# Three units in the first group of each exponential phase, in a kernel that runs window attention beside a feed-forward product

## The chip, the cores and the metric

One core of a Trainium2 chip runs the kernel. The time is the device time of one execution in microseconds, and lower is better. Three runs of the kernel before lie between 299.94 and 300.24 us, with a median of 300.06 us. The core has TensorE (PE in the profile, with its weight load PEld), VectorE (DVE), ScalarE (ACT), GpSimd (POOL) and SyncE (SP); the last two mainly issue transfers here.

## The reference

Attention over 8 batches of 8 heads, 576 positions and 64 numbers a head: each position sees itself and the 127 before it, with a bias that grows with distance by a slope of the head. The result, 4608 rows of 512, goes through `h = x @ w_in` (2048 wide), `g = h * cos(h)` and `g @ w_out`.

```python
scores = scale * np.matmul(q, k.transpose(0, 1, 3, 2))
mask = (rel >= 0) & (rel < window)                # window = 128
scores = np.where(mask, scores + bias[None], -1000000000.0)
...
attn = attn / (np.sum(attn, axis=-1, keepdims=True) + 1e-09)
x = np.matmul(attn, v) ...                        # 4608 x 512
h = x @ w_in
g = h * np.cos(h)
return (g @ w_out).astype(np.float32)
```

## The kernel before

The program is written as a list of operations, each with what it reads and writes. The operations of one engine run in an order that a table gives: `Plan.follow(TABLE)` unpacks a string into steps of 16 bits, one for each operation, and builds the order from them. For an operation that either ACT or DVE can do, the high bit says which. Semaphore waits come from what an operation reads and writes, so nothing runs ahead of its data, and an operation that waits holds up what is behind it on its engine.

The attention is cut into units. A unit (b, pair, G) is a batch, a pair of heads and one half (G = 0 or 1) of the first 512 positions; a unit (b, 't') is the last 64 positions of a batch for all heads. There are 72. Nine are done at the start. The rest is spread over six phases, which have 8, 10, 10, 12, 14 and 9 units; in each phase ACT loads the table of the exponential once, does the phase's units, and goes back to the cosine. Between and beside them run the feed-forward products of a block of 512 rows a phase.

A group of units goes through these steps:

- `scores` (L539, and L529 for a 't' unit): PE writes q·k of a unit into two banks of PSUM. One run holds the scores of all units of the group.
- `exps` (L598, L590): ACT takes the exponential of a unit into `p` or `ptail`.
- `mask` (L623, L611): DVE multiplies by `emask`, which holds bias and window (made by ACT at L460 from `dif`, which POOL makes).
- `pv` (L653, L656; L640, L642): PE multiplies by v into one bank of PSUM a unit.
- `norm` (L694, L696; L681, L684): DVE divides by the sums and writes `xnats`; in phase 5 `norm_two` (L710, L712) divides two units' sums at once.
- x is then transposed, either on PE (L742, into the bank that held the unit's sums, and copied out by ACT L752 or DVE L753 into `xT`) or by a DMA on SP.

The eight banks of PSUM are dealt out by name: 4 to 7 are `SB` (scores, and the first product of the feed-forward part), 2 and 3 are `UB` (sums with v, and the transposes of x), 0 and 1 are `OB` (second product). With two units in a group the scores take all four of `SB`.

The first product is L782 (L975 for the first block), its cosine is L787 on ACT and its product h·cos(h), `gT`, is L791 on DVE. The second product is L1161 (first block) and L1067; L1067 works on 256 columns and on sums `wsum` and `gsum` besides. Its results are copied from PSUM by ACT (L1052) or DVE (L1053) into `ob` and stored by SP. At the start, q and k of batch 0 are loaded, transposed on PE (L483) and copied into `qt` and `kt` by ACT (L500) and DVE (L501). From batch 2 on they are loaded by POOL and transposed by DMAs on SP (L396, L399). v is loaded at L375, `w_in` at L407, `w_out` at L413.

Of the kernel before, what the change touches and what calls it, by code (L numbers as in the profile page):

```python
# [37 lines left out]
    '!JB(zEKr!Mj%{>;HUNYjab!Z7$qCql;L3G!CjefR+FFk(bw73vr<2ntCbb8MB)_5dQYyf6J%<J=0tY;ul(MgN&rc'
    'O0s&EiG$uIcm#Y~Vab;v#yqnaVrE7GY>V-A}Btqa`;P_Nv&jvF#{*7WM`>VMkre&#)Wy?uO_aV#gax-'
    'm{4=v5trFP6j>R?Tw2c0rY#J*M(j<PaOY>o)>#w^hUa2)xJ2kX>J~-'  # L40
    '#3SczLYEI#)13`0UMgZCvSU&r@KXVhQx8AYHOt^~S#t385v1pL)39f1&X4(!RY_VSn%~;N7Le~0Vt5k)3C!7qncH'
    'Sb_KKyP6<WQBL=(H{om`}^2hwehkBNkN1f6-'
    '=6Jf`#n1*9F&|{#~8ip5b`?XFO3>mnmKg4fqM&X#D2BXTu`vb#MxEL-'
    '2=FZh<=U!>)?uhVjo~ev?pC0h90j^d!W2#$W>Vg}3Lez;yMB~`dF58D5!*GHZ4bkokcrZJo8XMBIs3+J`c0!*&!='
    'cNak2M(+9t6%k<c;_TI5&xT-;_~SjMe)zLQ?kr-'
    '9G)}so_oZgT~!nS)>B%(>F{i(nL<%Kma6dPT_kIY8xqVGm@6sSZY)QY;}3kyZHF!JjrNbPWohF6A1kpQae^Jz>4Y'
    'nMq|4ag_#Z%abX$X0Qx{bdg5-'
    'w!C^Sy0wzSSv6YO*7!5g5KOZPW>L)jeqDWi^PVfHiNt_&bV&I7<#pb?el1f*R3lvbBscPqQM6(|M=#E!7MQtWiEo'
    '^$q8jetWg{{laSk`ID;w6<lHL!It@CI3ZRWxET-dy=6bdfZi^BN)-'
    'kx6rkxYh^Af7Y$CX%W0qP@nf!;+_cuy#JAV$$(>L5)aS8M@n1a32RRL3Yb{W0a`!VJ8|o4{JEnxs(L});p(&v8a9'  # L50
    'u_yO{KZHL$YuW?tu(Sy-'
    '!vCGTmAdZpg4wXLtycpkG<<E5@OtDZg=!_1h1+Njmjw*z0aL)7QnhFOPv(elHPlI>oe%EXgvk}suL+RHI+l!oPEe'
    'ttc)y)KY7q-'
    'GO9HpEp~!82*s>_!_J5TR{@5f%EL7h^Wh(4l4fbO%j~jd783&`#My06C4>3;+Is6L%3tT|^hYe#$tr1&iB&6{dwW'
    'wmj!;Baz_4=p8Jja_9ps>tY{=<;GUvOwSAXGq+K`;>!KNrH|ImXY(ASTzHFN^apdvpSj*r6^VK)$8H@P=`NPcPO&'
    'XkYSBhFw`irt0gqb!LQPqlVQC7VwU?z)4yP6n<)+6xUk=rH29r)HJ=#nkkufV0J5o_@v9wsQWd0@&P$WT0e*0vOC'
    'WIl=#9la*x}LDtWaQG=0xl2(#f%Kz3QWi+K|tR$xwKh#_K~ywPUk>V_~X988-'
    'dL$7M*|kTUzrMQ~>ttJm@GYT>9QFLiQ#JGHIu^Q5UX9joXGsV+1N~s5tf4rg&Z0t843@yK)VUZ;eO{vvf>bj#_<{'
    'E{YJE13lG{)N}UY3D6Y>lsCkRX4ja{$9_e$IQETy;j`zD56VwIGwJ{vRRhIkkY72;<?OL;WxyDsbjLJ`d?#gik4L'
    '%OwvOj>3X-Yk5pe`ia}jeHouYwjx-lYe?zUO*6w~{=z!E<7?VOdoJcyIBk3;YN22T&Udsl*?z2EoT*eN`VQ(2lOw'  # L60
    '$ie!%Cd#CND}y^H-5G~apWoVM#%(x$>q1=4UeA7@v$>FHVpXpRNz-`z1w9-2S&rNI|0<^yIkuIxJ1&2qr-'
    'yn-P&*BAkwbEg<YgZWM`B<Ux7!?;yxT0hEB9Poq9_H<xB+6$<+&1*V*jXQ=!i##UhbBC-HxJ9b4f>O5FQM$GVlYY'
    '0;EzOMeT$+Oi@ir?~G>em;QF`Fb7Uw0-'
    ')DSUv5QX5E;wvHsQX@ok50m+CO*%wR0XM0gH$JNq(o?|pd}rcrfU%@Ny^NS$EwY}9WNlRrb}CwAb0!CyUIkX8zeE'
    't`lBMNi5`Z9289jS-byN0#8`Z0-K46!6u51NJvfI*I<pVOKD}#Bep<(EjKAJ>#OvyA?}aT-'
    'Eb<QtZWG>gAiq@nZu|-Z>5YIIxXgTPJ-Qv8(%8OF{x~utj?J<T~4~q=Mu!G!`B%o{U^X7EYfMjy|cFw5l`KlR}P!'
    'Ka8_mW<8uzKs|eA|5Ic*_e7cdlcU3q+K^v!GU5I4-4igxj^A<ASLge=;<iQSZL!w7=WR?W#-'
    'vXhCLeN@7x(>g+{qRDABl6lLS<Fw>!h`LQKaFe(HMu)ipAva=P&;AW;|7_8}?>Xa&1&CWqRI3oTyJm0VHkMj~b-'
    'KU~R;VLVn(IO$x|2XD-#Cwa~YvoxGM@0FUnOnlZXB(9|3jhMQu{ARUV7(DVnyPJ@o)_f&pP-'
    '0v1&I@q5tK0fHEZqW2B6vpePz;Nsr3p!)OwvLraMQ%IB0%b!Fk8kvD!^ICX(d5SU`>)JBl;A)3x!^A~*gA1H!Njk'  # L70
    '9bb31AJ#9jLnSFn5nJP8V+>6WI*{{9$K=-'
    'Ii4(}ekB>9rlTbz8;dAV@$vsGY#Mm*p3)v9cI)0mEeyn;9Sk1Ej+_{IEB=6m(OWM%qp|L4FkV=POcUwRSz4?%tjO'
    '!EE7%nJVFo1y$1xLEKDW3+%V*`a_(LEi!<eA{Ja22J?)4@RI|7PRIIN8a6UkTIrQNx^0MmIX}Gdse33v8*ibI3(}'
    'Q6!`hQq7VFL0TWDyL%1z)LEb|Fqa2QJsRyz<9M$)jGC(Gyq6mu#GUiIyWiMn}lrw_vC^2CnX65Kq(JOA5auqsW#('
    'az6gPr;3Fs3vS*iFTO!lleCE-fW~K`s@;f-'
    'DuL7*vWwMFvwo)YDYK%Ys!&lL=}a$qa_Dqe_$j$%4|P%7Sk&C^p7|E-05OoaEoQU{w(_HKhuIl)N)0L6E?If-ndQ'
    'f>bOkomPRMj6=zXYB;2Fs8S$=8>KAS9bxj%$jo92RQykW$_h$ynL-'
    ';1n|B~0C{NjJ5M;#~HD{_qDyS92ASr8Q=(}$hf?wlN8Dh7U35CEE3Rb4eZHcVrLB=YO&ys+EVM&F9-'
    '>_E|awkyN8>TE$>Y^ZLfm%hXRv?#4)t*Y5EYzr4%5w1xWK3uw7gWYn<tfyI;9|8HRZ>;#t145fwkp%W<gb}oO8Vt'
    ';%~TDI391Zd3iT@kVuEmcuME+!AOkCeh?Xh408{MGRAGcvK=>2_;SOCz;Xi5FXBMh@##BcNK~)Hu608vNLvl*BDH'  # L80
# [15 lines left out]
class Plan:  # L96
# [63 lines left out]
    def follow(self, text):  # L160


        raw = zlib.decompress(base64.b85decode(text))
        n, at, self.order = len(raw) // 2, 0, []
        assert n == len(self.all)
        for lo, hi in zip(raw[:n], raw[n:]):
            at = (at + lo + 256 * hi) % 65536
            o = self.all[at % 32768]
            if isinstance(o.fn, dict):
                e = "dve" if at >= 32768 else "act"  # L170
                o.fn, o.eng = o.fn[e], (e,)
            self.order.append(o)
# [80 lines left out]
def bass_alibi_sliding__then__act_gcu_kernel(  # L253
# [8 lines left out]
    with ExitStack() as ctx:  # L262
# [12 lines left out]
        JN, PRE2, SEEDN, XD, LORD = (5,), (), {}, {4: 6}, 0  # L275
        SDPRI, NH, LWPRI, G1, S4IN, SPLIT = 1, 2, 2, 1, True, True
# [3 lines left out]
        SB, UB, OB = [4, 5, 6, 7], [2, 3], [0, 1]  # L280

# [236 lines left out]
        def scores(us, slot):  # L518

            def f(e):  # L520
                ins = None
                for n, (b, pr, G) in enumerate(us, slot):
                    banks = SB[2 * n:2 * n + 2]
# [21 lines left out]
            for n, (b, pr, G) in enumerate(us, slot):  # L545
                for x in SB[2 * n:2 * n + 2]:
# [627 lines left out]
        def attention(us, phase):  # L1174

            for g in range(0, len(us), 2):
                two = us[g:g + 2]
# [5 lines left out]
                else:  # L1183
                    if g // 2 < SEEDN.get(phase, 0):
# [140 lines left out]
```

## Time and profile before

| | us |
|---|---|
| median of 3 runs | 300.06 |
| profiled execution | 299.71 |
| span of the profiled execution | 298.0 |
| TensorE busy | 287.9 |
| VectorE busy | 262.1 |
| ScalarE busy | 222.1 |
| GpSimd busy | 95.2 |

The span runs from the first to the last instruction of the execution; 1.71 us lie around it. Matmuls are pipelined and their ends are modelled: a matmul's busy time overlaps the next one's start. So the distance from start to start tells what a matmul takes, and the busy share tells only when TensorE had anything at all.

### The profile page before, as it was taken

Reading aid. Unit: us, or ns where it says so; the run is one execution under the profiler, and the core shown is the slowest. Engines: PE = TensorE matmul, PEld = TensorE weight load, DVE = VectorE, ACT = ScalarE, POOL = GpSimd, SP = SyncE. Lnnn points to the kernel's source line nnn. Section 1 sums busy time; section 2 is a strip of 40 time slices with the busy share of each in tenths; the row PEclk is TensorE's granted clock in tenths of the full one; section 3 lists DMA queues with packets and bytes.
Section 4 is the critical chain, followed back from the end, with each engine's and each line's share of the span. In section 5 each row is a group of like instructions: output and inputs, shape, how many; then the busy total and the mean of one; then the engine's idle time right before and its main releaser. Section 6 shows DMA issues by size and latency. Waiting matters only on the chain.

```text
span 298.0 us, 7278 instructions
## 1 busy us (share of the span) xinstructions
PE 287.9 (97%) x2974; PEld 205.2 (69%) x2974; DVE 262.1 (88%) x522; ACT 222.1 (75%) x318; POOL 95.2 (32%) x122
## 2 busy tenths in 40 slices
PE   2899999999999999999999999999999999999996
PEld 2678845446874586458854788547768888888884
DVE  3879877599977999899999999999999999999972
ACT  5788878689757889688777878579778758778620
POOL 7997000599642303991195005000000000000000
PEclk9999999999999999999999999999999999999999
DMA  7999999999999994999999939973131400041033
GB/s 153 173 205 208 207 169 146 180 196 155 136 175 147 130 187 90 142 173 173 169 170 133 163 85 130 159 164 74 21 79 21 150 2 0 2 141 37 10 134 106
DMA packets 147729, 37.96 MB, mean 127 GB/s; under 512 B 133360, under 2 KB 146416, under 8 KB 147696
## 3 DMA queue, kind: packets, MB, share of 16 engines
q0 software_dynamic: 99344, 18.10, 79.7%
q1 hardware_dynamic: 48352, 19.41, 34.5%
q8 instruction: 23, 0.38, 0.5%
q14 instruction: 10, 0.08, 0.1%
HBM read 36.70 MB, written 9.44 MB: 155 GB/s over the span
## 4 chain that ended last, share of the span: by engine, by line
PE 94%; DVE 2%; POOL 1%; issue 1%; ACT 1%; POOLq 0%; DVEq 0%
PE ps L1067 33%; PE ps L782 24%; PE ps L876 11%; PE ps L539 5%; PE ps L975 5%; PE ps L1161 4%; PE ps L653 3%; PE ps L656 2%; PE ps L742 2%; PE ps L483 2%; PE ps L529 1%; DVE kt L501 1%; PE ps L640 1%; PE ps L642 1%; PE ps L1138 1%
## 5 line engine op out<-in xcount | busy, mean ns | idle before, releaser
L1067 PE MATMUL ps<-w_outb,gT 128*128 128x256 f16 x512 | 82.3, 273 | 0.0
L782 PE MATMUL ps<-xT,w_inb 128*128 128x512 f16 x336 | 82.2, 379 | 0.0
L787 ACT ACTIVATE cos<-ps,halfpi 128x512 f32<-128x512 f32 x84 | 54.9, 687 | 18.9 <-PE ps L782 13.9
L598 ACT ACTIVATE p<-ps 128x768 bf16<-128x768 f32 (+1 forms) x64 | 55.6, 915 | 11.5 <-PE ps L539 9.5
L791 DVE TENSOR_TENSOR gT<-ps,cos 128x512 f16<-128x512 f32 x84 | 54.5, 686 | 5.5 <-ACT cos L787 5.1
L1067 PEld LDWEIGHTS ps<-w_outb,gT 128*128 128x128 f16 x512 | 48.2, 98 | 12.5 <-issue 1.3
L782 PEld LDWEIGHTS ps<-xT,w_inb 128*128 128x128 f16 x336 | 31.7, 98 | 31.1 <-DVE gT L791 1.5
L375 POOL DMA_DIRECT2D vp<-in_v_dram x40 | 34.3, 892 | 53.1 <-PE ps L656 35.3
L1067 PE MATMUL ps<-wsum,gsum 128*128 128x256 f16 x256 | 38.5, 273 | 0.0
L623 DVE TENSOR_TENSOR p<-p,emask 128x768 bf16<-128x768 bf16 (+1 forms) x64 | 38.0, 615 | 0.3
L385 POOL DMA_DIRECT2D qnat<-in_q_dram x30 | 25.5, 918 | 23.9 <-DMA qt<-qnat 23.9
L1052 ACT ACTIVATE ob<-ps 128x512 f32<-128x512 f32 x33 | 19.6, 598 | 13.7 <-PE ps L1067 11.2
L385 POOL DMA_DIRECT2D knat<-in_k_dram x30 | 25.7, 948 | 9.3 <-DMA kt<-knat 7.0
L1067 PEld LDWEIGHTS ps<-wsum,gsum 128*128 128x128 f16 x256 | 23.2, 98 | 4.0 <-issue 0.5
L876 PE MATMUL ps<-xT,w_inb 128*128 128x256 f16 x132 | 24.8, 273 | 0.0
L696 DVE TENSOR_TENSOR xnats<-ps,rec 128x256 f16<-128x256 f32 x56 | 21.9, 420 | 0.5
L539 PE MATMUL ps<-qt,kt 64*128 64x128 bf16 (+1 forms) x320 | 20.1, 253 | 1.3 <-DVE kt L501 1.3
L653 PEld LDWEIGHTS ps<-vp,p 128*128 128x128 bf16 x256 | 16.0, 99 | 4.3 <-issue 1.0
L653 PE MATMUL ps<-vp,p 128*128 128x65 bf16 x256 | 18.9, 196 | 0.1
L1067 PE MATMUL ps<-wsum,gT 128*128 128x256 f16 x112 | 18.1, 273 | 0.0
L539 PEld LDWEIGHTS ps<-qt,kt 64*128 64x128 bf16 x320 | 11.9, 98 | 8.6 <-issue 3.6
L1161 PE MATMUL ps<-w_outb,gT 128*128 128x512 f16 x64 | 17.6, 380 | 0.0
(111 smaller groups left out, 478.0 us busy)
## 6 DMA issues: line engine op xcount, KB each, us to landing
out_dram<-ob SPq DMA_DIRECT2D x35, 256.0 KB, 2.7
vp<-in_v_dram POOLq DMA_DIRECT2D x32, 128.0 KB, 6.9
qnat<-in_q_dram POOLq DMA_DIRECT2D x24, 128.0 KB, 7.1
knat<-in_k_dram POOLq DMA_DIRECT2D x24, 128.0 KB, 10.8
w_inb<-in_moe_w_in_dram POOLq DMA_DIRECT2D x4, 512.0 KB, 10.5
w_outb<-in_moe_w_out_dram POOLq DMA_DIRECT2D x4, 512.0 KB, 21.8
gsum<-in_q_dram POOLq DMA_DIRECT2D x1, 576.0 KB, 15.5
gsum<-in_k_dram POOLq DMA_DIRECT2D x1, 576.0 KB, 17.6
```

Of the source, the lines that this page charges most:

```text
L375: op("pool", [lambda e, t=t, rows=rows: e.dma_start(vp[b % 2][0:rows, t, :, 0:64], v[b, :, 128 * t:128 * t + rows, :].rearrange("h p d -> ...
L385: fns.append(lambda e, t=t, rows=rows: e.dma_start(nat[which][b % 2][0:rows, t, :, :], src[b, :, 128 * t:128 * t + rows, :].rearrange("h p ...
L539: ins = e.matmul(ps[:, banks[x], c0:c1], keys_ap(b, x, pr, kc), query_ap(b, x, pr, qb, 128 * nb), start=c0 == 0 and (b, pr, G) not in seed ...
L598: op("act", lambda e: e.activation(P[i][:, :, 0:hi], src_[:, :, 0:hi], ACTF.Exp, scale=0.125), w=held + [("P", i)], occ=920 if G else 691, ...
L623: op("dve", lambda e: e.tensor_tensor(p, p, m, ALU.mult), r=[("EM", h0), ("EM", h1)] + ([] if G else [("EM2", h1)]), w=[("P", i)], occ=600 ...
L653: ins = e.matmul(o, P[i][:, x, d0:d0 + 128], V[:, kc, h, 0:65], start=True, stop=not two)
L782: op("pe", lambda e, kc=kc: e.matmul(ps[:, bank, :], w_in[:, kc, 128 * fc:128 * fc + 128], xT[:, kc, r0:r0 + CH], start=(kc == 0), stop=(k ...
L787: op("act", lambda e: e.activation(cosb[ci][:, :], ps[:, bank, :], ACTF.Sin, bias=halfpi[:, 0:1]), r=["halfpi"], w=[("B", bank), ("cos", c ...
L791: op("dve", lambda e: e.tensor_tensor(gT[gi][:, fc, :], ps[:, bank, :], cosb[ci][:, :], ALU.mult), r=[("cos", ci)], w=[("B", bank), ("g", ...
L876: op("pe", lambda e, i=i, kc=kc: e.matmul(ps[:, bank, 256 * i:256 * i + 256], left(kc, p0 + i), right(kc), start=(start and i == 0 and kc ...
L1067: op("pe", lambda e, t=t, p=p: e.matmul(ps[:, bank, 256 * t:256 * t + 256], left(p, slice(128 * t, 128 * t + 128)), right(p), start=(start ...
L1161: op("pe", lambda e, t=t, fc=fc, bank=bank: e.matmul(ps[:, bank, :], gT[gi][:, fc, 128 * t:128 * t + 128], w_out[:, fc, :], start=(fc == 0 ...
```

## The change

The list `TRI` says with how many units each phase begins: three in phases 0 to 5, then two by two as before, and what is left over alone at the end. The third unit of a group has its scores in banks 2 and 3, since `SX` is `SB` with `UB` behind it. The products with v are done in twos (the first two units of a group of three, then the third alone). So the groups of phase 0 are 3, 2, 2, 1, those of phases 1 and 2 are 3, 2, 2, 2, 1, of phase 3 it is 3, 2, 2, 2, 2, 1, of phase 4 it is 3, five times 2, 1, and of phase 5 it is 3, 2, 2, 2. `follow` takes the first engine of an operation's own choice where the high bit isn't set. The table is another one throughout: it sets the order of all operations, those of the opening too, and which of ACT and DVE does a copy. The line numbers rise by 6 to 12.

```diff
 TABLE = (
-    'c-nPV2Y6If7JmPfH!Wo*A%PHdEHqifjs=k}tV#(GFqBXPBn4$bu`FK_%_4*%1ObV(K#D*JSt&-E!h-'
...
+    'c-n1N2S8M3w!R-T48s)afJhM)qwyIMOE#-'
...
             if isinstance(o.fn, dict):
-                e = "dve" if at >= 32768 else "act"
+                e = "dve" if at >= 32768 else o.eng[0]
                 o.fn, o.eng = o.fn[e], (e,)
...
+        TRI = {0:[3],1:[3],2:[3],3:[3],4:[3],5:[3]}
...
         SB, UB, OB = [4, 5, 6, 7], [2, 3], [0, 1]
+        SX = SB + UB
...
             def f(e):
                 ins = None
                 for n, (b, pr, G) in enumerate(us, slot):
-                    banks = SB[2 * n:2 * n + 2]
+                    banks = SX[2 * n:2 * n + 2]
...
                 keys += tkeys((b, pr, G))
-                held += [("B", x) for x in SB[2 * n:2 * n + 2]]
+                held += [("B", x) for x in SX[2 * n:2 * n + 2]]
...
         def exps(u, n, table):
             b, pr, G = u
-            banks = SB[2 * n:2 * n + 2]
+            banks = SX[2 * n:2 * n + 2]
...
         def attention(us, phase):
-            for g in range(0, len(us), 2):
-                two = us[g:g + 2]
+            sizes = TRI.get(phase, [])
+            sizes = sizes + [2] * ((len(us) - sum(sizes) + 1) // 2)
+            for i, size in enumerate(sizes):
+                g = sum(sizes[:i])
+                two = us[g:g + size]
...
-                    if g // 2 < SEEDN.get(phase, 0):
+                    if i < SEEDN.get(phase, 0):
...
-                sets = [list(zip(two, OB if phase < 0 and g == 0 else UB))]
+                sets = [list(zip(two[j:j + 2], OB if phase < 0 and g == 0 else UB))
+                        for j in range(0, len(two), 2)]
                 if any(u[1] == "t" for u in two):
-                    sets = [[s] for s in sets[0]]
+                    sets = [[s] for set_ in sets for s in set_]
```

Two places show how rows move. On PE in phase 0, from the first score run of the phase on, the kernel before has:

```order
L1161 MATMUL ps<-w_outb,gT 128x512 x7
L539 MATMUL ps<-qt,kt 128x256 x2
L539 MATMUL ps<-qt,kt 128x128 x2
L539 MATMUL ps<-qt,kt 128x256 x2
L539 MATMUL ps<-qt,kt 128x128 x2
L1161 MATMUL ps<-w_outb,gT 128x512 x15
L539 MATMUL ps<-qt,kt 128x256 x2
```

and the changed kernel has, at the same place:

```order
L1169 MATMUL ps<-w_outb,gT 128x512 x7
L547 MATMUL ps<-qt,kt 128x256 x2
L547 MATMUL ps<-qt,kt 128x128 x2
L547 MATMUL ps<-qt,kt 128x256 x2
L547 MATMUL ps<-qt,kt 128x128 x2
L547 MATMUL ps<-qt,kt 128x256 x2
L547 MATMUL ps<-qt,kt 128x128 x2
L1169 MATMUL ps<-w_outb,gT 128x512 x14
L547 MATMUL ps<-qt,kt 128x256 x2
```

The run of scores (two rows a unit) has a third unit, and 14 matmuls of the second product stand behind it in the place of 15. On ACT at the end of phase 2, from the phase's third pair of units on, the kernel before has exponentials `p` (L598; 128x1024 for a unit with G = 1, 128x2x384 for one with G = 0), copies of x (`xT`), the tail's exponential (`ptail`) and copies of results (`ob`) in this order:

```order
L1052 ACTIVATE ob<-ps 128x512
L752 ACTIVATE xT<-ps 128x256 x2
L598 ACTIVATE p<-ps 128x1024 x2
L752 ACTIVATE xT<-ps 128x256 x2
L598 ACTIVATE p<-ps 128x1024 x2
L752 ACTIVATE xT<-ps 128x256 x2
L590 ACTIVATE ptail<-ps 128x1024
L598 ACTIVATE p<-ps 128x2x384
L1052 ACTIVATE ob<-ps 128x512
```

The changed kernel has:

```order
L606 ACTIVATE p<-ps 128x1024
L760 ACTIVATE xT<-ps 128x256
L606 ACTIVATE p<-ps 128x1024 x3
L760 ACTIVATE xT<-ps 128x256
L598 ACTIVATE ptail<-ps 128x1024
L606 ACTIVATE p<-ps 128x2x384
L1060 ACTIVATE ob<-ps 128x512
L760 ACTIVATE xT<-ps 128x256
```

Three exponentials of 128x1024 stand in a row where pairs stood with copies of x between them.

More of the change, by code (lines that the diff above doesn't have):

```diff
@@ L38 @@
[L38 to L80, printed above, removed]
@@ new lines @@
+    'WioJtGa&r5$WjE`3X3Z2&5iFfpbDb=%JJuvAaZZ`Ds<(zspbD=6h{SaqPn}ZZC!U0fBcPjP>xLRj2SlbI`<-'
+    'E(Yj=gw4)InXrXl87c5=5qoL}HMr|s;o9oy3iL9Z(m3fobfj1Zkyg~l-}h?szQiLYFldX+b@h1kq-'
+    'V4+gBwks4WYk}+_3E-'
+    '$s74Qj>a)Rgsk7b!DHQjDwXlW9v3GU#g%K4aU%AGmkXdPF|5>$*{n_YdTmMkwshdAHdTxx(fMoDG_WFQ_Ba~{>AK'
+    '{F!`~6_(PSdWD+ODZxp(iOam*@JX(VFRLR|acblaNU)ZnPy8K=VIX7)%vnV)oE=7p&jYWJ-SOYS}K*1$`XtCu%jI'
+    'dOT?pQ-'
+    'Z<wY4~$RIs$DT0`&jwQGpGd$MQzE%kBd(%O|pB|ol+Pro>Q?}!hpJVjqkr1ep@AUL2CkN(o`I_qft*n3NgfVqOU;'
@@ L545, in scores @@
             for n, (b, pr, G) in enumerate(us, slot):
-                for x in SB[2 * n:2 * n + 2]:
+                for x in SX[2 * n:2 * n + 2]:
                     if (b, pr, G) not in seeded:
@@ L582, in exps @@
             b, pr, G = u
-            banks = SB[2 * n:2 * n + 2]
+            banks = SX[2 * n:2 * n + 2]
             held = [("B", x) for x in banks]
```

60 lines of the change are left out of this document (51 added, 9 removed).

## The prediction

> **What bounds the kernel.** I read the page first, then TensorE's busy time by stage, then the starts of its instructions, because busy time hides short stops here.
>
> ```profile
> span 298.0 us, 7278 instructions
> PE 287.9 (97%) x2974; PEld 205.2 (69%) x2974; DVE 262.1 (88%) x522; ACT 222.1 (75%) x318; POOL 95.2 (32%) x122
> ...
> PEclk9999999999999999999999999999999999999999
> ...
> PE 94%; DVE 2%; POOL 1%; issue 1%; ACT 1%; POOLq 0%; DVEq 0%
> ...
> 0.00:18.00 18.00, 11.03 (x161) 8.55 (x162) 12.07 (x36) 13.25 (x23) 16.42 (x29) 1.00 1.24 170
> 18.00:60.00 42.00, 41.92 (x452) 27.79 (x451) 32.13 (x72) 32.85 (x49) 15.78 (x19) 1.00 1.54 184
> 108.00:119.00 11.00, 11.00 (x171) 8.18 (x169) 10.10 (x27) 10.28 (x18) 2.36 (x3) 1.00 0.75 135
> 222.00:295.00 73.00, 73.00 (x665) 62.70 (x662) 66.49 (x94) 48.02 (x67) 0.00 (x0) 1.00 0.17 56
> ```
>
> PE is busy for 97% of the span at a full clock and carries 94% of the chain that ended last. The columns of the stage rows are the stage, its length and the busy time of PE, PEld, DVE, ACT and POOL: before 18 us PE idles 7 us of 18, and after that 0.08 us of 42 and nothing of 11 and of 73. Its work is the same in both kernels: the instruction lists have 2974 matmuls of the same shapes. So the change can only move the time through the opening, and through stops of PE after it. Those stops do not show as idle time, since a matmul's end is modelled and overlaps the next start. They show in the starts:
>
> ```profile
> 51.40 0.38 PE L782 MATMUL ps<-xT,w_inb 128*128 128x512 f16 x1
> 51.62 0.38 PE L1161 MATMUL ps<-w_outb,gT 128*128 128x512 f16 x1
> 52.04 0.19 PE L653 MATMUL ps<-vp,p 128*128 128x65 bf16 x1
> ...
> 48.54 0.39 PE L1161 MATMUL ps<-w_outb,gT 128*128 128x512 f16 x1
> 48.97 0.19 PE L653 MATMUL ps<-vp,p 128*128 128x65 bf16 x1
> ...
> 46.65 0.25 DVE L694 RECIPROCAL rec<-ps 128x4 f32<-128x4 f32 x2 [0.78 <-PE ps L656]
> 46.87 0.76 DVE L696 TENSOR_TENSOR xnats<-ps,rec 128x256 f16<-128x256 f32 x2
> 47.54 1.28 DVE L623 TENSOR_TENSOR p<-p,emask 128x1024 bf16<-128x1024 bf16 x2
> ```
>
> A 512-column matmul is followed after 0.22 us (51.40 to 51.62). Behind the ones at 51.62 and 48.54 the next start comes after 0.42 and 0.43: a stop of 0.21 each. The second ends 0.15 after VectorE's masks do (47.54 + 1.28 = 48.82), and those stood behind the normalisation of the group before. So the price of one visible stop is about 0.2 us, and a semaphore from DVE to PE costs about 0.15.
>
> **The change, part by part.** *Three units in the first group of phases 0 to 5, the third one's scores in banks 2 and 3.* No matmul, exponential, mask or store is added; the number of score runs on PE (37), of table loads (14) and of DMAs is the same in both lists. By count the cost is nothing, and what hides it is that PE does the same work; if a wait appears, the cover is gone. A wait that is possible: the third unit's scores hold the banks that the sums with v need next, so the group's first product waits until ScalarE's third exponential has read them. From below this costs nothing; from above, one exponential and its way back in each of six phases:
>
> ```profile
> L598 ACT ACTIVATE p<-ps 128x1024 bf16<-128x1024 f32 x32 | 31.3, 1021 | 5.8 <-PE ps L539 4.0 <-PE ps L656 1.0 <-PE ps L529 0.7
> L598 ACT ACTIVATE p<-ps 128x768 bf16<-128x768 f32 x32 | 24.5, 808 | 5.7 <-PE ps L539 5.5
> ```
>
> 0.81 + 0.15 = 0.96 us, six times: 5.8 us. I take nothing, because in phase 0 fourteen matmuls of 0.22 us (3.1 us; L1169 by the changed kernel's order) stand behind the triple's scores and ahead of the first product, which is longer than three exponentials of 0.81 (2.4 us) and a mask of 0.5. In phase 2 it is 28 matmuls of 256 columns.
>
> The Trainium skill speaks against this part: "Perfetto Trace Analysis", section on identifying performance opportunities, says that a repeated bubble on the engine that should be saturated can mean that SBUF or PSUM has no room for the next tile. By that page every phase would show such a bubble. The trace of before has no third unit in these banks and can't show it; the sum by the page would be that of the second rival below.
>
> *Phase 0.* Both stops above go. PE's order ahead of the products with v (L653) was as follows; L539 are scores, L742 transposes of x, L1161 the second product of the feed-forward part:
>
> ```order
> L1161 MATMUL ps<-w_outb,gT 128x512 x5
> L742 MATMUL ps<-ident,xnats 128x128 x2
> L1161 MATMUL ps<-w_outb,gT 128x512
> L742 MATMUL ps<-ident,xnats 128x128 x2
> L539 MATMUL ps<-qt,kt 128x256 x2
> L539 MATMUL ps<-qt,kt 128x128 x4
> L539 MATMUL ps<-qt,kt 128x256 x2
> L539 MATMUL ps<-qt,kt 128x128 x4
> L1161 MATMUL ps<-w_outb,gT 128x512
> L653 MATMUL ps<-vp,p 128x65
> ```
>
> In the changed kernel PE has the third unit's product in hand right after such a score run:
>
> ```order
> L547 MATMUL ps<-qt,kt 128x256 x2
> L547 MATMUL ps<-qt,kt 128x128 x4
> L547 MATMUL ps<-qt,kt 128x256 x2
> L547 MATMUL ps<-qt,kt 128x128 x4
> L661 MATMUL ps<-vp,p 128x65 x3
> L664 MATMUL ps<-vp,p 128x65
> L661 MATMUL ps<-vp,p 128x65
> L664 MATMUL ps<-vp,p 128x65
> L1169 MATMUL ps<-w_outb,gT 128x512 x2
> L750 MATMUL ps<-ident,xnats 128x128 x2
> L1169 MATMUL ps<-w_outb,gT 128x512 x2
> ```
>
> The next pair's masks get 2 + 2 + 3 matmuls of 0.22 us more ahead of their product. Two stops of 0.21 are gone, and I give back 0.1 because there VectorE normalises one unit alone and then the transposes wait on it: **−0.3 us** (bounds −0.6, if the smaller stops of 0.1 go too, and +0.3).
>
> *The opening.* DVE before (first fence) and now (second), from the first piece of `kt` (the transposed k) on; `emask` is the mask with the position bias, `p` the exponentials:
>
> ```order
> L501 COPY kt<-ps 128x4x32x4
> L465 COPY emask<-emask 128x2x128 x3
> L623 TENSOR_TENSOR p<-p,emask 128x2x384 x2
> L501 COPY qt<-ps 128x4x32x5
> L501 COPY kt<-ps 128x4x32x5 x2
> ```
>
> ```order
> L509 COPY kt<-ps 128x4x32x4
> L473 COPY emask<-emask 128x2x128 x2
> L631 TENSOR_TENSOR p<-p,emask 128x2x384
> L473 COPY emask<-emask 128x2x128
> L631 TENSOR_TENSOR p<-p,emask 128x2x384
> L447 CAST ident<-ident 128x128
> L509 COPY kt<-ps 128x4x32x5 x2
> ```
>
> The second copy of `qt` has gone from DVE to ACT, and the pieces of the mask are spread. The rows give start and busy time in us; the last one gives the us from the first load's issue to its landing. What that costs and frees is read here:
>
> ```profile
> 9.25 2.35 PE L483 MATMUL ps<-ident,gsum 128*64 128x128 bf16 x40
> 13.50 1.04 PE L539 MATMUL ps<-qt,kt 64*128 64x256 bf16 x12 [0.38 <-DVE kt L501]
> 17.96 0.94 PE L975 MATMUL ps<-xT,w_inb 128*128 128x256 f16 x7
> 11.06 0.82 DVE L501 COPY qt<-ps 128x640 bf16<-128x640 bf16 x1
> 11.79 1.57 DVE L501 COPY kt<-ps 128x640 bf16<-128x640 bf16 x2
> 12.07 1.51 ACT L598 ACTIVATE p<-ps 128x768 bf16<-128x768 f32 x2 [0.62 <-PE ps L539]
> 8.15 0.78 POOL L407 DMA_DIRECT2D w_inb<-in_moe_w_in_dram  x1
> 8.90 0.92 POOL L375 DMA_DIRECT2D vp<-in_v_dram  x1
> ...
> w_inb<-in_moe_w_in_dram POOLq DMA_DIRECT2D x1, 512.0 KB, 7.9
> ```
>
> PE's transposes end at 11.60, so the copies of `kt` can move up by at most 11.79 − 11.60 = 0.19, and the scores of 13.50, which waited for them, with them. ACT gets 0.8 us more, of which its idle 0.62 hides most. On POOL a load of v is now ahead of the first load of `w_in`, which moves that issue from 8.15 by 0.92 to about 9.1; PE's first use is at 17.96, and the load's row of 7.9 us to landing puts it at 17.0. That is covered by 0.9 us, and if the cover goes PE waits for what the load is late. I take **−0.2 us** (bounds −0.4 and +0.3).
>
> *End of phase 2*, where the eighth unit and the tail now share the last pair and one unit stays alone. In the trace of before, ACT and PE run there so:
>
> ```profile
> 111.64 0.62 PE L539 MATMUL ps<-qt,kt 64*128 64x256 bf16 x12
> 112.19 0.28 PE L1067 MATMUL ps<-wsum,gsum 128*128 128x256 f16 x1
> 112.86 1.15 PE L1067 MATMUL ps<-wsum,gsum 128*128 128x256 f16 x9
> 113.84 0.28 PE L742 MATMUL ps<-ident,xnats 128*128 128x128 f16 x2
> 113.95 0.38 PE L1067 MATMUL ps<-wsum,gsum 128*128 128x256 f16 x2
> 112.30 1.94 ACT L598 ACTIVATE p<-ps 128x1024 bf16<-128x1024 f32 x2 [0.23 <-PE ps L539]
> 114.15 0.71 ACT L752 ACTIVATE xT<-ps 128x256 f16<-128x256 f16 x2
> ```
>
> ACT before (first fence) and now (second):
>
> ```order
> L752 ACTIVATE xT<-ps 128x256 x2
> L598 ACTIVATE p<-ps 128x1024 x2
> L752 ACTIVATE xT<-ps 128x256 x2
> L590 ACTIVATE ptail<-ps 128x1024
> L598 ACTIVATE p<-ps 128x2x384
> ```
>
> ```order
> L606 ACTIVATE p<-ps 128x1024 x3
> L760 ACTIVATE xT<-ps 128x256
> L598 ACTIVATE ptail<-ps 128x1024
> L606 ACTIVATE p<-ps 128x2x384
> L1060 ACTIVATE ob<-ps 128x512
> ```
>
> PE now has there:
>
> ```order
> L537 MATMUL ps<-qt,kt 128x64 x16
> L1075 MATMUL ps<-wsum,gsum 128x256 x3
> L750 MATMUL ps<-ident,xnats 128x128 x2
> L1075 MATMUL ps<-wsum,gsum 128x256
> L750 MATMUL ps<-ident,xnats 128x128 x2
> L1075 MATMUL ps<-wsum,gsum 128x256 x3
> L661 MATMUL ps<-vp,p 128x65
> ```
>
> The copies of x that stood between the pairs of exponentials are down to one, and it stands behind three of them; on PE the tail's scores end a shared score run. The third exponential of ACT's row of three waits for this score run's end; the copy of x behind it frees bank 3, and the product L661 needs that bank. ACT's way: 0.11 to start (112.19 to 112.30) + 0.97 (1.94 for two) + 0.36 (0.71 for two) + 0.15 back = 1.59 us. PE's own work until then: seven matmuls of 0.11 (0.98 for nine) and two pairs of transposes of 0.11, 0.98 us. PE stops for **+0.6 us** (bounds 0, if the score run ends while ACT is still behind and the next work is short, and 0.65 with a second semaphore in the wait). Behind it are queued ACT's tail exponential and the last unit's, so phase 3's first matmuls don't gain.
>
> *Other places.* ACT's and DVE's orders change in every phase: at the ends of phases 3 and 4, `w_in` products stand close behind the last exponentials, and phase 5 normalises one pair fewer jointly. No row of before shows these; two more stops of the size seen at 48.97, **+0.4 us** (bounds −0.3, where stops of before go, and +1.0).
>
> Sum: −0.3 − 0.2 + 0.6 + 0.4 = +0.5 us. Against the profiled execution's 299.71 (1.71 outside its span of 298.0) that is 300.2; the median of the runs shown, 300.06, is 0.35 above that execution, so on medians 300.6.
>
> **The rivals.** *Gains alone.* Opening and phase 0 hold and the stop in phase 2 doesn't come, since ACT reaches its third exponential early or PE has more in hand: −0.3 − 0.2 and up to −0.3 elsewhere, −0.7: 299.4. For it speaks that PE's stops of 0.2 in phase 0 are plainly there to be had; against it, ACT's row of three. It ends faster, and it decides as soon as PE has 0.6 us more work at that place.
>
> *Banks held.* The third unit holds banks 2 and 3 where less work than in phase 0 stands behind its scores: two phases uncovered at 0.96 give +1.9, with the +0.5 then 302.4; all six give 305.8.
>
> *A late load.* The first `w_in` slice, or a transposed `qt`/`kt` behind a store on SP's queue, lands 1 us late: 301.6. Against it: 0.9 us of cover at the first use.
>
> *Nothing happens.* The new stops cancel the old: 300.1; it is within the forecast's own range.
>
> **How the numbers follow.** Forecast 0.48 (own range 299.9 to 301.3), gains alone 0.24, banks held 0.16, a late load 0.12. The range takes in the gains at 299.3 and the banks' two-phase case to 302.2. A measurement of this kernel tells about 0.2% (0.6 us) from no change. Faster than 299.46: 0.20 of the gains and 0.02 of the forecast. Slower than 300.66: 0.16 + 0.11 of the rivals and 0.15 of the forecast. The rest, 0.36, is the same.
>
> **What would show it.** Right: two fewer gaps of 0.42 between the starts of L1169 and L661 at 45 to 55 us; a gap of about 0.6 ahead of an L661 at about 115 us, with ACT's copy L760 ending just before; scores at 13.3 instead of 13.50. Wrong: gaps of about 1 us ahead of the first L661 of each phase (banks); PE idle ahead of the first L983 (load); or a second stop in phases 3 to 5 larger than 0.4.

## The result, and the profile after

The changed kernel takes 301.65 us (median of 4 runs, 301.39 to 301.82), the kernel before 300.10 us in the same series (299.94 to 300.24): a ratio of 1.0051, 95% interval 1.0034 to 1.0069. It is slower by 1.55 us. The forecast was 300.6 us with a range of 299.3 to 302.2, so the time lies within the range, and the forecast loss of 0.5 us was a third of what came. The forecast's own range, 299.9 to 301.3, ends below the measured time. The profiled execution took 301.52 us, 1.81 more than that of before.

The page of the changed kernel's profile, and TensorE's busy time by stage (stage, length, busy us of PE, PEld, DVE, ACT and POOL):

```profile
span 299.8 us, 7296 instructions
PE 288.7 (96%) x2974; PEld 203.6 (68%) x2974; DVE 262.1 (87%) x522; ACT 221.3 (74%) x320; POOL 95.0 (32%) x122
...
PEclk9999999999999999999999999999999999999999
...
0.00:18.00 18.00, 10.58 (x164) 7.95 (x165) 11.47 (x34) 13.48 (x25) 16.47 (x29) 1.00 1.26 173
18.00:60.00 42.00, 41.85 (x449) 26.95 (x448) 31.20 (x70) 33.05 (x52) 15.97 (x20) 1.00 1.56 177
108.00:119.00 11.00, 10.65 (x155) 7.39 (x156) 9.87 (x31) 7.76 (x12) 1.68 (x2) 1.00 1.83 182
```

The work and the clock are those of before, and TensorE is still busy nearly all the time. Behind the opening, most of the idle time that was not there is in the stage from 108 to 119 us, 0.35 us of 11. The other stages behind it have 0.14 us or less of new idle time, and before 18 us TensorE idles 0.45 us more than before (10.58 busy us against 11.03).

To place the rest I compared the starts of TensorE's matmuls at the same amount of its own work. Both kernels have the same 2974 matmuls, so each was given its price from start to start (0.216 us with 512 columns, 0.109 with 256, 0.030 for a product with v, 0.056 for a transpose of x, 0.054 and 0.027 for scores), and the two traces were set against each other where the sums are equal. At the times of the table, both have also started the same number of matmuls of each shape, so the prices have no part in it. How far the changed kernel is behind (us, worked out from the starts in the two traces):

| up to | time in the kernel before | behind | of it in this part | the prediction's term |
|---|---|---|---|---|
| opening | 29.5 | +0.04 | +0.04 | -0.2 |
| phase 0 | 60 | -0.29 | -0.33 | -0.3 |
| phase 1 | 94 | +0.04 | +0.33 | other places |
| phase 2 | 131 | +0.90 | +0.86 | +0.6 |
| phase 3 | 161 | +1.15 | +0.25 | other places |
| phase 4 | 202 | +1.16 | +0.01 | other places |
| phase 5 | 241 | +1.62 | +0.46 | other places |
| end | 294.5 | +1.91 | +0.29 | other places |

The other places sum to +1.3, and the prediction had +0.4 for them.

The stops that the prediction named, in TensorE's starts. Phase 0, where before 0.42 and 0.43 us lay between two starts:

```profile
53.03 0.38 PE L1169 MATMUL ps<-w_outb,gT 128*128 128x512 f16 x1
53.39 0.19 PE L661 MATMUL ps<-vp,p 128*128 128x65 bf16 x1
...
47.28 0.81 PE L1169 MATMUL ps<-w_outb,gT 128*128 128x512 f16 x3
48.12 0.25 PE L661 MATMUL ps<-vp,p 128*128 128x65 bf16 x3
...
48.54 0.38 PE L1169 MATMUL ps<-w_outb,gT 128*128 128x512 f16 x1
48.85 0.34 PE L547 MATMUL ps<-qt,kt 64*128 64x256 bf16 x4
```

Both stops are still there, a little shorter. Ahead of 53.39 it is 0.15 us (0.36 where 0.22 is the price); ahead of 48.12 it is 0.19 (three products take 0.65 of the 0.84 us from 47.28 on). What has gone are two stops of 0.11 us ahead of transposes, at 44.99 and 53.49 us in the kernel before. In all, the stops of phase 0 fall from 0.68 to 0.38 us. The 0.31 us from 48.54 to 48.85 holds no stop: 0.09 of it is what TensorE takes at the entry of each run of 64-row matmuls (scores, or transposes of the tail). Entry and exit together cost 0.20 to 0.22 us beyond the matmuls' own prices in most score runs of both traces.

The end of phase 2, TensorE, ScalarE and VectorE:

```profile
114.29 0.28 PE L750 MATMUL ps<-ident,xnats 128*128 128x128 f16 x2
114.41 0.49 PE L1075 MATMUL ps<-wsum,gsum 128*128 128x256 f16 x3
115.24 0.20 PE L661 MATMUL ps<-vp,p 128*128 128x65 bf16 x1 [0.34 <-ACT xT L760]
...
113.89 1.02 ACT L606 ACTIVATE p<-ps 128x1024 bf16<-128x1024 f32 x1 [1.14 <-PE ps L537]
114.81 0.38 ACT L760 ACTIVATE xT<-ps 128x256 f16<-128x256 f16 x1
115.07 1.03 ACT L598 ACTIVATE ptail<-ps 128x1024 bf16<-128x1024 f32 x1
...
113.26 0.25 DVE L702 RECIPROCAL rec<-ps 128x4 f32<-128x4 f32 x2 [0.19 <-PE ps L664]
113.48 0.75 DVE L704 TENSOR_TENSOR xnats<-ps,rec 128x256 f16<-128x256 f32 x2
```

Three products of 0.109 from 114.41 on would let the product with v start at 114.74; it starts at 115.24, right behind ScalarE's copy (114.81 + 0.38 = 115.19). That is the forecast stop, 0.50 us where 0.6 was forecast, with the releaser that was named. But the rows also show what the forecast chain had left out. VectorE normalises until 114.23, the transposes of what it wrote start at 114.29, and the copy reads them: ScalarE's exponential, which makes way at 114.81, is only a little later than the copy's own data.

The rival of the held banks is answered by the same trace. In phases 1 and 2 TensorE runs from its last products into the first product with v without a stop:

```profile
74.20 0.49 PE L1075 MATMUL ps<-wsum,gsum 128*128 128x256 f16 x3
74.53 0.19 PE L648 MATMUL ps<-vp,ptail 128*128 128x65 bf16 x1
...
107.92 0.50 PE L1075 MATMUL ps<-w_outb,gT 128*128 128x256 f16 x3
108.26 0.23 PE L661 MATMUL ps<-vp,p 128*128 128x65 bf16 x2
```

Three products take 0.33 us of both 0.33 and 0.34. Over the six phases the gap ahead of the first product behind a group of three is 0, 0, 0, 0.01, 0.01 and 0.11 us above its price. The rule of the Trainium skill ("Perfetto Trace Analysis", identifying performance opportunities), by which the taken banks would show as a repeated bubble, has no repeated bubble here to explain. The 0.11 us in phase 5 stays open: the third exponential ends at 210.43 there and the second unit's mask at 210.44, and the product starts at 210.68, so either can have held it.

### The profile page after: what moved, and what is told of

It is laid out like the page before. It is cut to its first block, busy times and chain, and to the rows that moved or that the text cites. A ratio compares the mean times of both kernels' runs of the same rounds, so it can differ in the third digit from the quotient of the medians.

```text
span 299.8 us, 7296 instructions
## 1 busy us (share of the span) xinstructions
PE 288.7 (96%) x2974; PEld 203.6 (68%) x2974; DVE 262.1 (87%) x522; ACT 221.3 (74%) x320; POOL 95.0 (32%) x122
## 4 chain that ended last, share of the span: by engine, by line
PE 93%; DMA 3%; ACT 2%; issue 1%; DVE 1%; POOL 1%; ACTq 0%; POOLq 0%
PE ps L1075 32%; PE ps L790 24%; PE ps L884 11%; PE ps L547 5%; PE ps L1169 5%; PE ps L983 5%; PE ps L661 3%; DMA gsum<-in_k_dram 3%; PE ps L664 2%; PE ps L750 2%; PE ps L491 1%; ACT p L606 1%; PE ps L537 1%; PE ps L648 1%; PE ps L650 1%; PE ps L1146 1%
## 5 line engine op out<-in xcount | busy, mean ns | idle before, releaser
L1075 PE MATMUL ps<-w_outb,gT 128*128 128x256 f16 x512 | 81.6, 273 | 0.1
L795 ACT ACTIVATE cos<-ps,halfpi 128x512 f32<-128x512 f32 x84 | 54.0, 686 | 18.9 <-PE ps L790 15.2
L606 ACT ACTIVATE p<-ps 128x768 bf16<-128x768 f32 (+1 forms) x64 | 55.8, 918 | 13.3 <-PE ps L547 8.3
L1075 PEld LDWEIGHTS ps<-w_outb,gT 128*128 128x128 f16 x512 | 48.6, 98 | 11.4 <-ACT ob L1060 0.8
L1075 PE MATMUL ps<-wsum,gsum 128*128 128x256 f16 x256 | 41.4, 273 | 0.0
L1075 PEld LDWEIGHTS ps<-wsum,gsum 128*128 128x128 f16 x256 | 23.9, 98 | 4.3 <-issue 0.6
L1060 ACT ACTIVATE ob<-ps 128x512 f32<-128x512 f32 x31 | 18.5, 598 | 10.9 <-PE ps L1075 10.6
L704 DVE TENSOR_TENSOR xnats<-ps,rec 128x256 f16<-128x256 f32 x58 | 23.1, 420 | 1.0
L547 PE MATMUL ps<-qt,kt 64*128 64x128 bf16 (+1 forms) x320 | 19.3, 249 | 1.4 <-DVE kt L509 1.1
L1075 PE MATMUL ps<-wsum,gT 128*128 128x256 f16 x112 | 20.3, 273 | 0.0
L661 PEld LDWEIGHTS ps<-vp,p 128*128 128x128 bf16 x256 | 15.8, 98 | 6.4 <-issue 1.8
L661 PE MATMUL ps<-vp,p 128*128 128x65 bf16 x256 | 19.2, 195 | 0.6 <-ACT xT L760 0.3
L664 PE MATMUL ps<-vp,p 128*128 128x65 bf16 x192 | 17.7, 194 | 0.0
```

Of the source, the lines that this page charges most:

```text
L547: ins = e.matmul(ps[:, banks[x], c0:c1], keys_ap(b, x, pr, kc), query_ap(b, x, pr, qb, 128 * nb), start=c0 == 0 and (b, pr, G) not in seed ...
L606: op("act", lambda e: e.activation(P[i][:, :, 0:hi], src_[:, :, 0:hi], ACTF.Exp, scale=0.125), w=held + [("P", i)], occ=920 if G else 691, ...
L661: ins = e.matmul(o, P[i][:, x, d0:d0 + 128], V[:, kc, h, 0:65], start=True, stop=not two)
L795: op("act", lambda e: e.activation(cosb[ci][:, :], ps[:, bank, :], ACTF.Sin, bias=halfpi[:, 0:1]), r=["halfpi"], w=[("B", bank), ("cos", c ...
L1075: op("pe", lambda e, t=t, p=p: e.matmul(ps[:, bank, 256 * t:256 * t + 256], left(p, slice(128 * t, 128 * t + 128)), right(p), start=(start ...
```

## The experiments

Where a table of the order is transplanted, each operation keeps the order of the kernel that its part is taken from; behind the seam, the rest follows the other kernel's order. "Behind" is always TensorE's lag against the kernel before, worked out as above. The line numbers of these kernels lie up to 15 below those of the changed kernel, since their tables are shorter in lines: L1064 is its L1075, L739 its L750, L650 its L661.

**First four: which phase holds the loss.** The theory was that single stops of the new order cost the time, most of it in phase 2; the rival, that each group of three costs the same. Each `+` line is one kernel.

```diff
-        TRI = {0:[3],1:[3],2:[3],3:[3],4:[3],5:[3]}
+        TRI = {2:[3]}          # phase 2 alone; the order of before, of the changed kernel in phase 2, of before
+        TRI = {3:[3],4:[3],5:[3]}   # phases 3 to 5; the order of before, then of the changed kernel
+        TRI = {0:[3]}          # opening and phase 0; the order of the changed kernel, then of before
+        TRI = {0:[3],1:[3],3:[3],4:[3],5:[3]}   # all but phase 2
```

> The kernel before, with the changed kernel's three-unit group and its order in phase 2 alone (from that phase's first score run to the first one of phase 3). If the loss sits in single stops of the new order, most of it at the end of phase 2, this is slower than before by 0.9 us (0.6 to 1.2), with a gap of 0.5 us ahead of one product with v near 114 us. If every three-unit group costs the same by holding the banks of the sums (1.55 us over six phases), it is slower by 0.26 us.

> The kernel before up to the first score run of phase 3, and from there on the changed kernel's groups and order. Single stops: slower than before by 1.0 us (0.7 to 1.3), made up of 0.3 in phase 3, 0.1 in phase 4, 0.4 in phase 5 and 0.2 near 285 us. Same cost for every three-unit group: slower by 0.78 us, 0.26 in each of the three phases and nothing after them.

> The changed kernel's opening and phase 0 (groups and order), and from the first score run of phase 1 on the kernel before. Single stops: faster than before by 0.3 us, since two stops of 0.21 us ahead of products with v go. Same cost for every three-unit group: slower by 0.26 us.

> The changed kernel with phase 2 alone taken back to the groups of two and the order of the kernel before. Single stops: faster than the changed kernel by 0.9 us, so 0.65 us slower than before. Same cost for every three-unit group: faster than the changed kernel by 0.26 us, so 1.3 us slower than before.

| kernel | median us | ratio to before, 95% interval |
|---|---|---|
| phase 2 alone | 303.30 | 1.0105 (1.0088 to 1.0123) |
| phases 3 to 5 | 302.12 | 1.0069 (1.0052 to 1.0087) |
| opening and phase 0 | 300.49 | 1.0025 (1.0009 to 1.0041) |
| all but phase 2 | 302.13 | 1.0069 (1.0053 to 1.0085) |

All four totals miss both expectations. The lag says why: the seams cost time of their own. With phase 2 alone, TensorE falls back 1.1 us just behind the first seam and 1.2 us behind the second. With all but phase 2, and with phases 3 to 5, it falls back about 1.6 us behind the seam ahead of phase 3 (stops of 1.02 and 0.58 us in both). The totals therefore settle nothing. What lies between the seams does. From 104 to 119.5 us of the kernel before, where all three have started the same number of matmuls of each shape, the lag goes

| kernel | at 104 | at 119.5 | change |
|---|---|---|---|
| changed kernel | +0.03 | +0.89 | +0.86 |
| phase 2 alone | +1.51 | +2.38 | +0.87 |
| all but phase 2 | +0.10 | +0.10 | 0 |

So the loss came with phase 2's groups and order to 0.01 us, and went with them. In the same way phase 5 and the end cost +0.45 and +0.30 in the kernel with phases 3 to 5 (+0.46 and +0.29 in the changed kernel), and phase 0 gave -0.34 with the opening and phase 0 alone (-0.33). Phase 3's part can't be told from its seam's. Equal costs for each group of three do not show: the parts range from -0.33 to +0.86.

One trace doesn't fit: with the opening and phase 0 alone, TensorE has two stops of 0.24 and 0.29 us, at 133 and 224 us, where the order is that of the kernel before and where that kernel has none. They make up most of this kernel's loss, and their cause is open.

**Is phase 0's gain lost only at the seam?** Two more transplants changed over at other places.

```diff
         TRI = {0:[3]}
-        order of the changed kernel up to phase 1's first score run
+        order of the changed kernel up to its 541st operation (first kernel), its 475th (second)
```

> The changed kernel's opening and phase 0 again, but changed over to the kernel before where the two orders differ least, ahead of phase 1's first score run, so that fewer instructions stand at another place at the seam. The first transplant of phase 0 was 0.50 us ahead at 65 us and lost it again within phase 1, behind the seam. If the seam alone took it back, this is faster than before by 0.3 to 0.5 us; if what phase 0 gains is always owed to phase 1, it is the same as before within 0.2 us.

> The changed kernel's opening and phase 0, changed over to the kernel before right behind phase 0, where the two orders differ in two loads of v and a few products only (at the last seam an addition of weight sums on VectorE stood ahead of the products that phase 1's first scores waited for, 1.8 us). If the seam took the gain back: 0.2 to 0.5 us faster than before at the end, with phase 0's 0.2 us kept from 50 us to the end. If phase 1 takes it back without such a seam: same as before.

301.45 us (ratio 1.0046, 1.0029 to 1.0063) and 302.13 us (1.0055, 1.0031 to 1.0078). The second kernel's executions lie between 300.13 and 303.31 us and its trace is of one of 300.40, so the trace doesn't explain its median. Phase 0 gained 0.35 us in both, and both lost it again before phase 1 was done: 1.70 us at phase 1's first scores in the first, where TensorE waited for a product of VectorE, and 0.9 us at 62 to 69 us in the second, in two waits for the same kind of product. The rows of the waits of TensorE, first kernel and then second:

```profile
PE ps L522 <- DVE gT L784: 1.8, 1, 1.8
```

```profile
PE ps L775 <- DVE gT L784: 0.4, 1, 0.4
PE ps L522 <- DVE gT L784: 0.3, 1, 0.3
```

Neither expectation is met. Phase 0's gain is there in four of four traces, and I found no way to keep it; in the changed kernel itself phase 1 gives 0.33 us back. Part of that has a place. The four 64-row transposes of the tail stood inside a run of scores before (first fence), and stand alone now (second):

```profile
75.69 0.23 PE L729 MATMUL ps<-ident,xtail 64*128 64x64 f16 x2
75.73 0.28 PE L539 MATMUL ps<-qt,kt 64*128 64x256 bf16 x1
```

```profile
76.32 0.49 PE L1075 MATMUL ps<-w_outb,gT 128*128 128x256 f16 x3
76.74 0.29 PE L737 MATMUL ps<-ident,xtail 64*128 64x64 f16 x4
76.96 0.39 PE L1075 MATMUL ps<-w_outb,gT 128*128 128x256 f16 x2
```

Three products end their turn at 76.65, so the transposes take 0.31 us, of which four times 0.03 are their own. The other 0.2 us is the entry and exit of one more 64-row run.

**The stop at the end of phase 2.** Three edits of the changed kernel. The first gives TensorE five more products ahead of the stop and moves an addition of VectorE out of the way; the second is the same with that addition moved less far; the third puts ScalarE's copy ahead of the exponential.

```diff
 PE, between the products with v of units 1, 2 and of units 6, 7
-  10 products, transpose, 1, scores, product with v of unit 3, ..., transposes, 3 products
+   5 products, transpose, 1, scores, product with v of unit 3, ..., transposes, 8 products
 DVE
-  add, norm unit 1, norm unit 2, mask, norm unit 2, mask, norm unit 3    # a norm: reciprocal, then product
+  norm unit 1, norm unit 2, mask, norm unit 2, mask, norm unit 3, add      # first
+  norm unit 1, add, norm unit 2 ...                                        # second
```

```diff
 ACT
-  L606 p   (third in the row)
   L760 xT
+  L606 p
```

> The changed kernel; in phase 2 five of TensorE's 256-column products (5 x 0.109 us) move from ahead of the third unit's product with v to behind the last transposes ahead of the product that stopped for 0.50 us at 114.6 us, and one addition of VectorE (0.69 us) moves behind the normalisation of the third unit. If the stop is there because too little work stands between two products that share banks 2 and 3, the stop falls to 0.1 or less and the kernel is 0.3 to 0.5 us faster than the changed kernel. If ScalarE's chain alone sets that time, the stop moves with it and nothing is gained.

> As the repair of phase 2 before, with VectorE's addition moved by one normalisation only, so that TensorE's products don't wait for it (1.3 us there the last time). If the stop of 0.50 us comes from too little work between two products that share banks 2 and 3, it falls to 0.1 or less, and phase 2 ends 0.4 to 0.6 us earlier than in the changed kernel. If not, phase 2 ends as late as before the repair.

> The changed kernel; at the end of phase 2 ScalarE copies x (L760) ahead of the third exponential in its row, not behind it. The prediction's chain had 0.97 us of that exponential in it: by it the stop of 0.50 us goes. By the trace of the changed kernel the transposes that the copy reads end only about 0.2 us before the exponential does: then the stop falls by 0.1 to 0.2 us, and the exponential's delay comes back at the products behind it, so that the time to the end of phase 2 changes by less than 0.3 us.

| kernel | us | stop ahead of the product | phase 2 in all |
|---|---|---|---|
| changed kernel | 301.65 | 0.50 | +0.86 |
| five products, first | 302.53 (ratio to before 1.0100, 1.0073 to 1.0126) | 0 | +2.07 |
| five products, second | 301.57 (1.0049, 1.0033 to 1.0065) | 0 | +1.10 |
| copy ahead | 301.78 (a single execution) | 0.44 | +1.50 |

The first attempt is spoiled by its own side effect: TensorE's products waited 1.3 us for the moved addition. The second is the clean one. The stop is gone, and nothing is gained. TensorE's starts there:

```profile
108.50 0.71 PE L1064 MATMUL ps<-wsum,gsum 128*128 128x256 f16 x5
109.40 0.28 PE L739 MATMUL ps<-ident,xnats 128*128 128x128 f16 x2 [0.19 <-DVE xnats L693]
...
110.92 0.93 PE L1064 MATMUL ps<-wsum,gsum 128*128 128x256 f16 x7
111.95 0.29 PE L739 MATMUL ps<-ident,xnats 128*128 128x128 f16 x2
```

Five products from 108.50 take 0.55 us, and the transposes start after 0.90: a stop of 0.35, with VectorE's normalisation as releaser. Seven from 110.92 take 0.76, and the next start comes after 1.03: 0.26. With others of 0.11 at 109.84, 0.21 at 110.80 and 0.20 at 117.09, the stops sum to 1.13 us where the changed kernel has 0.10, 0.09, 0.50 and 0.18, in sum 0.87. The five products came out of the rounds before, and the stops appeared there. (A round is product with v, normalisation, transpose, copy, next product.) So it is not the work at that one place that is short: each round has the other engines' time in it, and within this stretch TensorE waits for them at one place or another. More work for TensorE from outside the stretch was not tried.

The third edit shows that the exponential is not the main cause of the stop. ScalarE waits for the transposes before it can copy (first fence; TensorE in the second, VectorE in the third):

```profile
114.18 0.38 ACT L749 ACTIVATE xT<-ps 128x256 f16<-128x256 f16 x1 [1.87 <-PE ps L739]
114.46 1.02 ACT L595 ACTIVATE p<-ps 128x1024 bf16<-128x1024 f32 x1
```

```profile
113.98 0.49 PE L1064 MATMUL ps<-wsum,gsum 128*128 128x256 f16 x3
114.74 0.19 PE L650 MATMUL ps<-vp,p 128*128 128x65 bf16 x1 [0.28 <-DVE xT L750]
```

```profile
113.04 0.76 DVE L693 TENSOR_TENSOR xnats<-ps,rec 128x256 f16<-128x256 f32 x2
113.71 0.68 DVE L620 TENSOR_TENSOR p<-p,emask 128x1024 bf16<-128x1024 bf16 x1
114.31 0.28 DVE L750 COPY xT<-ps 128x256 f16<-128x256 f16 x1
```

The stop shrank by 0.06 us only. VectorE's copy is its releaser now; it ends at 114.59, 0.03 us behind ScalarE's, and VectorE goes from normalisation through a mask to this copy without a pause. In the changed kernel the same copy ended at 115.03, 0.16 us ahead of ScalarE's. And the late exponentials cost 0.53 us at the first products of `w_in` behind it.

**Does the third unit in the sums' banks cost anything?** In phase 2 the group of three becomes two and one, with the products with v as they were.

```diff
-        TRI = {..., 2:[3], ...}
+        TRI = {..., 2:[2,1], ...}    # the third unit's score run 12 products later, in banks 4 and 5
```

> The changed kernel; in phase 2 the third unit's scores are a run of their own, 12 products behind the pair's, in the banks of the scores, so that they hold no bank of the sums with v. If holding those banks costs time, phase 2 gets faster than in the changed kernel. If it costs nothing (the first product with v comes 4 us behind these scores), phase 2 gets slower by the price of one more score run, 0.2 us, and the stop near 114.6 us stays at 0.5.

302.62 us, a single execution, of which 0.8 us is a late load at the opening (below). Against the changed kernel, the lag grows by 0.27 us at the added score run and by nothing else in the phase: the stop stays at 0.50. Holding the banks costs nothing in this phase, and the group of three saves a score run at that place. Over the whole phase both kernels have five runs, so the saving is given back by the group of one at its end.

**One round fewer.** A group of three gives its third unit a product of its own, so banks 2 and 3 are taken and given back seven times in phase 2 and not six (42 times and not 38 over the six phases).

```diff
-                sets: units 1 2 | 3 | 4 5 | 6 7 | 8 | tail | 10
+                sets: units 1 2 | 3 4 | 5 6 | 7 8 | tail | 10       # phase 2 only
```

> The changed kernel, with the three-unit group kept, but in phase 2 the products with v go in twos across the groups (units 1 and 2, 3 and 4, 5 and 6, 7 and 8), so that banks 2 and 3 are taken and given back six times and not seven. If the number of these rounds sets the loss, phase 2 loses less than the changed kernel's 0.9 us against the kernel before, by 0.3 us or more. If the order on the engines sets it and not the count, it loses as much or more, since this order is made from the changed kernel's with small moves.

304.67 us, a single execution: phase 2 lost 3.3 us in place of 0.86. VectorE was late in several rounds:

```profile
PE ps L739 <- DVE xnats L693: 1.1, 3, 0.4
PE ps L650 <- DVE xT L750: 1.0, 1, 1.0
```

With masks, normalisations and copies moved together by hand, the order was worse, and it says nothing of what a round fewer is worth in a good order. The count of rounds is not shown as the cause: phases 0, 2, 3 and 5 have one more round, and their parts are -0.33, +0.86, +0.25 and +0.46; phases 1 and 4 have none, and lost 0.33 and 0.01.

**The late load at the opening.**

```diff
 POOL (kernel before)
-  v, v, v, w_in 0, v, w_in 1
+  v, v, w_in 0, v, v, w_in 1
```

> The kernel before, with the first slice of w_in loaded ahead of the third block of v and not behind it. In several profiles TensorE waited 0.4 to 1.2 us near 17 us for that slice. If the late slice costs time in most executions, this is faster than the kernel before by 0.2 to 0.5 us; if other work near 17 us is as late, it is the same.

299.63 us, ratio 1.0002 (0.9990 to 1.0014): the same. In its trace TensorE still waits 0.3 us for that slice. Nothing here beats the kernel before.

## Why the prediction was right or wrong

*The frame.* That TensorE's work is the same, so that only stops and the opening count, held: busy 287.9 and 288.7 us, the clock full in both, and the whole difference can be laid out as lag.

*The range.* That 301.65 lies in it is in part luck. The forecast's own range ends at 301.3; the upper end of 302.2 was there for the banks' two-phase case, which did not happen (and which the rival's own sum puts at 302.4). The late load's 301.6 is nearest to the measured time, by chance: the changed kernel's profiled execution, 301.52 us, has no wait for that load.

*Phase 0, -0.3.* The size came right, -0.33, and the step did not: "Two stops of 0.21 are gone" is not what the rows show. They are still there with 0.19 and 0.15 us, and the gain comes for the larger part from two smaller stops of 0.11, which the text had only in its lower bound.

*The opening, -0.2.* Not shown. Scores expected at 13.3 came at 13.71 in the profiled execution, and the part measured +0.04. The number of score runs is 37 in both, as the text says, but not place by place: the opening has six and not five (0.2 us more by the price above), and phase 5 four and not five. The opening also differs from execution to execution of the same instructions. In the ten traces that have the changed opening it stands between -0.41 and +0.86 us at 29.5 us against the one trace of the kernel before; seven lie between -0.41 and +0.04 (mean -0.12), and the three above +0.6 are those in which TensorE waited for the first slice of `w_in`:

```profile
18.15 0.28 PE L972 MATMUL ps<-xT,w_inb 128*128 128x256 f16 x1 [1.15 <-DMA w_inb<-in_moe_w_in_dram]
```

(the kernel with the score run split off). So the rival of a late load at this use was real and priced well at about 1 us (waits of 0.9 to 1.2); the cover of 0.9 us, worked out from one landing time, was not there in three of ten. The kernel before's own opening has it too, with 0.4 and 0.6 us in two traces.

*The end of phase 2, +0.6.* The place and the size of the stop were right (0.50), and the transplants show that the loss belongs to this phase. The mechanism was named only in part. The step that failed is "ACT's way: 0.11 to start + 0.97 + 0.36 + 0.15": ScalarE's copy does end last in the changed kernel, but the exponential ahead of it adds only 0.06 us, since with the copy ahead of it the stop is still 0.44. What sets the rest is the round of product with v, normalisation on VectorE, transposes, copies, next product, with a mask of VectorE ahead of its copy. And the term stopped at one stop, where the phase lost 0.86: there are three smaller ones (0.10, 0.09 and 0.18 us, each ahead of transposes), where the kernel before has two in this phase (0.13 and 0.08). The rest is in stops below 0.05 us.

*Other places, +0.4.* This is the term that was mis-sized most: +1.3, in five parts of 0.01 to 0.46. "Two more stops of the size seen at 48.97" had no row behind the two. The bound of +1.0 was too low as well. The largest part, phase 5, is made of stops ahead of products with v, 0.11, 0.18, 0.13 and 0.28 us at 210.68, 214.18, 216.50 and 220.11 us; two of them:

```profile
213.78 0.38 PE L1075 MATMUL ps<-w_outb,gT 128*128 128x256 f16 x2
214.18 0.25 PE L661 MATMUL ps<-vp,p 128*128 128x65 bf16 x3
...
219.62 0.38 PE L884 MATMUL ps<-xT,qnat 128*128 128x256 f16 x2
220.11 0.19 PE L648 MATMUL ps<-vp,ptail 128*128 128x65 bf16 x1
```

Two products take 0.22 of these 0.40 and 0.49 us. The score run that phase 5 saves takes about 0.2 us off the sum. The end's part is one stop of 0.26 at 285.03 us. None reaches the 0.4 us that the text named as a sign of being wrong; what each of them waits for was not settled.

*The banks.* Costing them at nothing was right, up to the 0.11 us in phase 5, for the reason given: first products start 3.7 to 4.8 us behind the start of the triple's last score matmul.

*Gains alone, 0.24.* The point from which it decides, more work for TensorE at the end of phase 2, was tried with work out of the rounds before: the stop goes and the time stays.

What stays open is whether the groups of three or the new table's order cost the time. Every transplant carries both. What is shown is where it went: 0.86 us in phase 2, which follows that phase's groups and order, and the rest in parts of up to 0.46 us, with 0.2 us of phase 1's part in one more 64-row run.

## What to carry to other kernels

Where an engine's busy time is near 100%, compare two traces by its start times at equal work, at points where both have started the same number of instructions of each shape: totals of 0.5% split into places, and most effects of 0.1 us reproduced here from kernel to kernel although the times of executions scatter by ten times that. When a forecast sum comes right, look at its terms in the rows all the same: phase 0's did, by other stops than those it was made of. A stop at the end of a chain that goes around several engines wasn't cured here by giving the waiting engine work out of the rounds before; the time showed up there. And where a forecast has a remainder of "other places", go through the order for them, since they outweighed the large one here. One kind could have been counted ahead of any run: each separate run of 64-row matmuls costs about 0.2 us, and the two lists show how many each phase has.

## What was not expected of the hardware

Most traces repeat far more closely than the times. Behind the opening, two executions of the same order keep their distance within 0.01 to 0.05 us for long stretches. For instance, the kernel with the earlier load stands at -0.28 us against the kernel before at 20 us and at -0.26 at 294 us, and the kernel with the copy ahead stands at -0.47 us against the changed kernel at 21 us and at -0.43 at 113 us. The two stops of 0.24 and 0.29 us described above are the exception. Between these traces, the differences that don't come from the order lie mostly in the first 21 us. Whether that also holds for the scatter between executions of one program (299.5 to 301.1 us for the kernel before, 300.1 to 303.3 for the second kernel with another seam) isn't shown, since each kernel has one trace. Against a simple late transfer as its cause, moving that transfer's issue ahead by one load changed nothing that 12 executions can tell.
